# An S4 convolution and local attention kernel: its convolution kernel generated in quarters of the channels, from one written list of steps

## The chip, the core and the metric

The kernel runs on one core of a Trainium2 chip. The core has a matrix engine (PE, with a weight-load path shown as PEld), a vector engine (DVE), an activation engine (ACT), a general engine (POOL) and a sequencer that mostly issues DMAs (SP). Each engine works through its own queue in order; engines wait for each other through semaphores. On-chip memory is SBUF (128 partitions) and PSUM, where matmuls accumulate. The metric is device time in microseconds (us); smaller is better.

## The reference

Four layers on x of shape (1, 2048, 512), all bf16: S4 convolution, local attention, and both again with the same weights.

```python
def _A_ref(u, A_re, A_im, B_re, B_im, C_re, C_im, log_dt, Dskip):
    dt = jnp.exp(log_dt)[:, None]
    logdA = dt * (A_re + 1j * A_im)
    l = jnp.arange(L).astype(A_re.dtype)                      # bf16 positions
    P = jnp.exp(logdA[:, :, None] * l[None, None, :])
    K = jnp.einsum("dn,dnl,dn->dl", Cc, P, dt * Bc).real      # (512 channels, 2048 lags)
    y = irfft(rfft(pad(u)) * rfft(pad(K)))[:L]
    return y + u * Dskip

x = x + _A_ref(_layernorm(x), ...)
x = x + _B_ref(_layernorm(x), B_wqkv, B_wo)   # 32 heads, 8 keys at distance 0, 2, .., 14
x = x + _A_ref(_layernorm(x), ...)
x = x + _B_ref(_layernorm(x), B_wqkv, B_wo)
```

The positions are rounded to bf16, so that far lags fall together: the distinct ones are u + 8v with 21 values of u (`U_POS`) and 32 of v, and K at those is a product of two small tables of powers of lambda = exp(dt A).

## The kernel before, in words

The span has five parts: kernel generation (`kgen`), then for each of two layers the convolution (`a_layer`) and the attention (`b_layer`, whose order comes from a planner, `Plan`; it is not touched).

**Kernel generation.** `_kgen_ladder` (L564) makes lambda (`LAM`) and squares it eleven times: ACT squares (`sq`, L624), DVE makes the new imaginary (L632) and real part (L633, `lad`), ACT casts to bf16 (`L`, L626 to L629), with the eight instructions of C times B (`cb`) between. Each power is [128 modes, 2 parts, 512 channels].

Then two tables are built by doubling, for half of the channels at a time (256 channels, as 128 pairs): `Utab` (cb times lambda to the power u, steps 4, 2, 1, 256, 1024, 512, 2048) and `Vtab` (lambda to the power 8v, steps v2, v4, v8, v16, where step m makes entries m+1 to 2m-1 from 1 to m-1). `cmul` (L326) makes one step: four DVE products into `cp` (L336), then two sums. For half 0 most sums are made on PE (`add`, L487: identity matmuls into `psadd`, with a minus through `nident`) and evicted by ACT (L495); for half 1 the sums are DVE's (L345). The copies of powers into the tables (L417) and of cb (L383) are DVE's for half 0 and ACT's for half 1.

`products(c, U)` (L422) multiplies V by U for a quarter c of 128 channels: per pair of channels two matmuls of 64 weight columns by 42 (L432), real and imaginary part, and one per eight pairs that adds Dskip at lag 0 (L438). ACT casts the result to `KT` (L440); DMAs turn it to `rows` with lags on partitions (L446; eight per quarter, on SP for c of 0 and 1, half on POOL for 2 and 3).

`spectrum` (L452) multiplies rows by the constant `G`, in four blocks of 1024 frequencies and ten matmuls, for quarters 0 and 1; ACT casts to `ks` (L459), a DMA writes it to `kt_scratch` in DRAM. `spectrum_pairs` (L463), for quarters 2 and 3, uses that frequency f and its partner 1024 further differ in the sign of the odd lags alone: even lags (four matmuls) and odd lags (one) go to two banks, ACT copies the odd ones (L472), DVE writes sum and difference (L474).

The first layer norm's sums run on ACT, two passes of 16 rows (L175), spread through the steps; DVE applies it (L194).

**First stage and convolution, layer 0.** `first_stage` (L222) transforms the normed rows: two matmuls per row j against `F1` (L231), evicted to `Z` by ACT, for odd j half by DVE (L238 to L241). It takes turns with the last spectrum blocks on PE. `a_layer`'s loop then runs over 16 groups of 32 channels: transpose Z on PE (L202), evict `zt` on DVE (L207), second stage `xp` (L214), cast `xc` on ACT (L291), multiply by the spectrum `Kt` on DVE into `pab` (L298), inverse second stage `vp` on PE (L281), cast `VT` on ACT (L283). `load_k` (L260) loads Kt from `kt_scratch`, two DMAs of 256 KB per group on SP, into four buffers; group cg+4 is asked for after pab of cg. F1T (1 MB) is loaded on SP at the loop's start (L305). `y_rows` (L311) ends the convolution with `ps_y` matmuls (L317).

Order: outside the regions called `manual_schedule` a scheduler places the instructions; inside them, the order is that of the program text. Matmuls on the convolution's path wait for Z, Kt and PSUM buffers.

Of the kernel before, what the change touches and what calls it, by code (L numbers as in the profile page):

```python
# [12 lines left out]
ALU = mybir.AluOpType  # L13
# [54 lines left out]
P0 = U_POS.index(0)  # L68


def _kernel_dft():

    lag = np.arange(S)
    pos = lag.astype(np.float32).astype(NPBF).astype(np.int64)
    f = (np.arange(128)[None, :] * 2 + 1 + 512 * np.arange(16)[:, None]).reshape(-1)
    row = {}
    for s, u in enumerate(U_POS):  # L80
        for v in range(NV if s < NU - 1 else 1):
            row[u + 8 * v] = s * NV + v
    G = np.zeros((6 * 128, 2, S), dtype=np.float64)
    ang = -2 * np.pi * ((lag[:, None] * f[None, :]) % 8192) / 8192.0
    idx = np.array([row[p] for p in pos])
    np.add.at(G[:, 0, :], idx, np.cos(ang))
    np.add.at(G[:, 1, :], idx, np.sin(ang))
    G = G.reshape(6, 128, 4, 1024)
    return np.transpose(G[:5], (2, 1, 0, 3))
# [79 lines left out]
def first_norm_stats(nc, small, eps, Xg):  # L169

    st = {n: small.tile([128, NJ], F32, name="n1_" + n, bufs=1) for n in ("sum", "nmean", "m2", "den", "rstd", "nb")}
    junk = small.tile([128, D], BF, name="n1_junk", tag="junk", bufs=1)

    def row(j, func, out, **kw):
        nc.scalar.activation(junk[:], Xg[j // 4][:, j % 4, :], func, accum_out=st[out][:, j:j + 1], **kw)  # L175

    def ops():
        for j in range(NJ):
            yield row(j, ACT.Identity, "sum")
        nc.scalar.activation(st["nmean"][:], st["sum"][:], ACT.Copy, scale=-1.0 / D)  # L180
        for j in range(NJ):
            yield row(j, ACT.Square, "m2", bias=st["nmean"][:, j:j + 1])
        nc.scalar.activation(st["den"][:], st["m2"][:], ACT.Ln, bias=eps[:], scale=1.0 / D)
        nc.scalar.activation(st["rstd"][:], st["den"][:], ACT.Exp, scale=-0.5)
    return st, ops()


def first_norm_scale(nc, st):
    nc.vector.tensor_tensor(st["nb"][:], st["nmean"][:], st["rstd"][:], ALU.mult)


def first_norm_apply(nc, st, Xg, Ng):
    for j in range(NJ):
# [27 lines left out]

def first_stage(nc, tc, C, Ng, Z):  # L222

    turns = [C["psk_end"]] + [C["psg"][i][1] for i in range(8, 15)]
    nexts = {2 * i + 1: 8 + i for i in range(8)}
    with tc.tile_pool(name="a_ps1", bufs=2, space=PSUM, reuse_waits="tile") as ps1:
        for j in range(NJ):
            ps = ps1.tile([128, 2, D], F32, name="ps_s1", tag="ps1")
            with tc.issue_after(turns[j // 2].ins):
                for r in range(2):  # L230
                    mm = nc.tensor.matmul(ps[:, r, :], C["F1"][:, j, r, :], Ng[j // 4][:, j % 4, :], start=True, stop=True)  # L231
            if j in nexts:
                tc.add_manual_dep(C["psg"][nexts[j]][0].ins, mm.ins.name,
                                  mybir.DependencyInfo(mybir.DependencyClass.NoSync, mybir.DependencyReason.DATA),
                                  reason="spectrum and first stage by turns")
            src = ps[:].rearrange("k r (c e g) -> k r c g e", c=16, e=GE)
            if j % 2 == 1:
                nc.scalar.copy(z_view(Z)[:, 0, j], src[:, 0])  # L238
                nc.vector.tensor_copy(z_view(Z)[:, 1, j], src[:, 1])
            else:  # L240
                nc.scalar.copy(z_view(Z)[:, :, j], src)  # L241


def a_layer(nc, tc, C, Xg, Ng, kt_dram, load_w, Z, es_z):

    with ExitStack() as es:
        es.enter_context(es_z)
        layer = 0 if Z is None else 1
        def pool(name, bufs=1, es=es, **kw):
            return es.enter_context(tc.tile_pool(name=name, bufs=bufs, reuse_waits="tile", **kw))  # L250
        if layer == 0:
            Z = pool("a_z").tile([128, NGR, 128], BF, name="Z")
# [7 lines left out]
        def load_k(cg):  # L260
            Kt = fwork.tile([128, 8, 2, 128], BF, name="Kt", tag="Kt", bufs=4)
            rows = kt_dram.ap()[:, cg * 32:(cg + 1) * 32].rearrange("k (e g) a l -> k e (g a l)", e=GE)
            for h in range(2):
                nc.sync.dma_start(Kt[h::2].rearrange("q g a l -> q (g a l)"), rows)
            kts[cg] = Kt

        for cg in range(4):
            load_k(cg)
        if layer == 0:
            first_stage(nc, tc, C, Ng, Z)  # L270
# [15 lines left out]
        with tc.manual_schedule():  # L286
            for cg in range(-2, 18):
# [4 lines left out]
                if cg + 2 < 16:  # L292
                    zts[cg + 2] = z_transposed(nc, P, C, Z, (cg + 2) * 8)
# [32 lines left out]
def cmul(nc, tb, out, a, m, e, hn, add=None):  # L326

    cols = hn * e * 2  # L330
    prod = {}
    for i in range(2):
        for r in range(2):
            k = (i * 2 + r) * cols
            prod[i, r] = tb[:, k:k + cols]
            nc.vector.tensor_tensor(prod[i, r].rearrange("n (h e t) -> n h e t", h=hn, t=2), a(r),  # L336
                                    m[:, i].unsqueeze(2).to_broadcast([128, hn, e, 2]), ALU.mult)
    last = None
    for r, (x, y) in enumerate((((0, 0), (1, 1)), ((1, 0), (0, 1)))):
        o = out(r)  # L340
        if add is not None:
            add(r, prod[x], prod[y], o)
        else:
            x, y = (prod[k].rearrange("n (h f c) -> n h f c", h=hn, f=o.shape[2]) for k in (x, y))
            last = nc.vector.tensor_tensor(o, x, y, ALU.add if r else ALU.subtract)  # L345
    return last


def kgen(nc, tc, C, prm, kt_dram, load_rest, norm_stats, norm_apply):
    with ExitStack() as es:  # L350
        wk = es.enter_context(tc.tile_pool(name="k_work", bufs=1, reuse_waits="tile"))
        lp = es.enter_context(tc.tile_pool(name="k_powers", bufs=1, reuse_waits="tile"))
        vp = es.enter_context(tc.tile_pool(name="k_v", bufs=1, reuse_waits="tile"))
        gp = es.enter_context(tc.tile_pool(name="k_g", bufs=1, reuse_waits="tile"))
        Lb = {p: lp.tile([128, 2, D], BF, name=f"L{p}") for p in (1, 2, 4, 8, 16, 32, 64, 128, 256, 512, 1024, 2048)}
        cb = lp.tile([128, 2, D], BF, name="cb")
        V = vp.tile([128, DH2, 2, NV, 2], BF, name="Vtab")
        nc.gpsimd.memset(V[:, :, 0, 0, :], 1.0)
        nc.gpsimd.memset(V[:, :, 1, 0, :], 0.0)
        Gt = [gp.tile([128, 5, 1024], BF, name=f"G{b}") for b in range(3)]  # L360
        u0_es = ExitStack()
        up, late = [None, None], []

        def power(p, dsl):
            return Lb[p][:, :, dsl].rearrange("n r (h t) -> n r h t", t=2)

        with tc.tile_pool(name="k_prep", bufs=1) as pp:
            raw, load = load_raw(nc, pp, prm)
            _kgen_ladder(nc, tc, C, cb, Lb, pp, raw, load)
        g3 = es.enter_context(tc.tile_pool(name="k_g3", bufs=1, reuse_waits="tile"))  # L370
        Gt.append(g3.tile([128, 5, 1024], BF, name="G3"))
        load_rest()
        for b in range(4):
            nc.sync.dma_start(Gt[b][:], C["G_h"].ap()[b])
        kp = es.enter_context(tc.tile_pool(name="k_kp", bufs=2, reuse_waits="tile"))
        up[1] = es.enter_context(tc.tile_pool(name="k_u1", bufs=1, reuse_waits="tile"))
        up[0] = u0_es.enter_context(tc.tile_pool(name="k_u0", bufs=1, reuse_waits="tile"))
        cp = wk.tile([128, 8192], BF, name="cp")
        psk_pool = es.enter_context(tc.tile_pool(name="k_psk", bufs=2, space=PSUM, reuse_waits="tile"))

        def u_start(half):
            U = up[half].tile([128, DH2, 2, UW, 2], BF, name="Utab", tag="Utab")
            (nc.scalar.copy if half == 1 else nc.vector.tensor_copy)(U[:, :, :, P0, :].rearrange("n h r t -> n r h t"),  # L383
                                  cb[:, :, half * 2 * DCH:(half + 1) * 2 * DCH].rearrange("n r (h t) -> n r h t", t=2))
            return U

        def u_mul(half, U, p, src, dst, h0=0, h1=DH2, tb=cp, add=None):

            e = src[2]
            f = len(dst)  # L390
            step = dst[1] - dst[0] if f > 1 else e

            def a(r):
                return U[:, h0:h1, r, src[0]:src[0] + (e - 1) * src[1] + 1:src[1], :]

            def out(r):
                return U[:, h0:h1, r, dst[0]:dst[0] + f * step, :].rearrange(
                    "n h (f s) t -> n h f s t", s=step)[:, :, :, 0:e // f, :].rearrange("n h f s t -> n h f (s t)")
# [20 lines left out]

        quarters = ((0, DH2 // 2), (DH2 // 2, DH2))  # L420

        def products(c, U):  # L422

# [858 lines left out]
```

## Time and profile before

| what | us |
| --- | --- |
| median of 3 runs | 467.61 (467.24 to 468.58) |
| the profiled execution | 466.74 |
| its span, first to last instruction | 464.9 |
| busy in the span: PE, DVE, ACT | 386.4, 414.3, 335.2 |
| end of lambda (LAM) to the last spectrum output | 10.35 to 136.2 |
| first xc to first ps_y, layer 0 | 137.5 to 174.7 |
| the same in layer 1 | 307.58 to 341.11 |

The profile is one execution, recorded by hardware. Times of instructions are from the span's start. A group of instructions is told by its line, engine, operation and tiles with their busy time, count and mean duration, and then the idle time of the engine just before them with what ended it. A mean duration includes the last part in which the next instruction has begun already, so instructions that follow each other start at shorter distances than their durations. The granted clock of PE is a share of full speed.

### The profile page before, as it was taken

How to read it: one execution, taken by the hardware profiler on the slowest of the kernel's cores; microseconds unless marked ns; L12 is line 12 of the kernel's file. 1: busy time of each engine (PE TensorE's matmuls, PEld its weight loads, DVE VectorE, ACT ScalarE, POOL GpSimd, SP SyncE). 2: the span in 40 equal slices, each digit the busy share in tenths (PEclk: the TensorE clock that was granted, in tenths of full speed). 3: DMA queues.
4: the chain of work that ended last, by engine and by line, in shares of the span. 5: the costliest groups of instructions: out<-in, count | busy, mean ns of one | idle time of the engine just before them, and what ended most of it. 6: DMA issues, size and time to landing. Idle time of an engine off the chain costs nothing.

```text
span 464.9 us, 11615 instructions
## 1 busy us (share of the span) xinstructions
PE 386.4 (83%) x4692; PEld 259.1 (56%) x4731; DVE 414.3 (89%) x857; ACT 335.2 (72%) x579; POOL 19.4 (4%) x51
## 2 busy tenths in 40 slices
PE   2006789979977989999998899879988999988996
PEld 1002349466335864567776665347745567876662
DVE  4899999999786987879999999989879899999990
ACT  6987997984867898965665369969978656752354
POOL 3000000002300000001001000000000000110000
PEclk9999995878999899999999899999999999996899
DMA  8940001333579991002507007128700000456022
GB/s 237 420 159 0 1 1 17 83 69 83 137 170 276 274 287 36 3 3 59 102 1 161 2 1 221 54 52 273 222 0 5 1 1 3 99 103 118 1 92 92
DMA packets 36618, 45.56 MB, mean 98 GB/s; under 512 B 26660, under 2 KB 28068, under 8 KB 35668
## 3 DMA queue, kind: packets, MB, share of 16 engines
q1 hardware_dynamic: 34500, 41.00, 31.5%
q0 software_dynamic: 1248, 2.63, 2.6%
q10 hardware_dynamic: 816, 1.18, 0.7%
q8 instruction: 37, 0.61, 0.6%
q14 instruction: 17, 0.14, 0.1%
HBM read 30.55 MB, written 6.29 MB: 79 GB/s over the span
## 4 chain that ended last, share of the span: by engine, by line
PE 41%; DVE 31%; ACT 15%; issue 6%; DMA 5%; SPq 1%; DVEq 0%; ACTq 0%
PE ps_qk L900 10%; DVE prodpv L1054 9%; DVE cp L336 7%; DVE prodqk L929 4%; PE Lp L946 3%; ACT xc L291 3%; PE ps_v L961 3%; DMA Kt<-kt_scratch 3%; PE vp L281 3%; PE ps_o L1088 2%; PE pt L202 2%; PE xp L214 2%; ACT Z L1114 2%; PE po L1062 2%; DMA V<-V 2%
## 5 line engine op out<-in xcount | busy, mean ns | idle before, releaser
L929 DVE TENSOR_TENSOR prodqk<-qT,N 128x1024 bf16<-128x1024 bf16 (+3 forms) x176 | 83.8, 541 | 4.7 <-ACT qT L902 2.7
L1054 DVE TENSOR_TENSOR prodpv<-V,Lsb 128x1024 bf16<-128x1024 bf16 (+1 forms) x168 | 81.8, 558 | 0.2
L900 PE MATMUL ps_qk<-xnT,wqk 128*128 128x512 bf16 x256 | 61.4, 379 | 1.1 <-ACT xnT L886 1.1
L1062 PE MATMUL po<-halves,prodpv 128*128 128x64 bf16 x1024 | 48.4, 201 | 3.5 <-DVE prodpv L1054 2.0
L1062 PEld LDWEIGHTS <-prodpv 128*128 128x128 bf16 x1024 | 40.7, 103 | 17.3 <-DVE prodpv L1054 9.6
L298 DVE TENSOR_TENSOR pab<-xc,Kt 128x2048 bf16<-128x2048 bf16 x32 | 39.1, 1223 | 9.7 <-ACT xc L291 5.4
L493 PE MATMUL psadd<-cp,sb_ident 128*128 128x512 bf16 (+3 forms) x48 | 18.4, 383 | 33.2 <-DVE cp L336 30.2
L291 ACT CAST xc<-xp 128x1024 bf16<-128x1024 f32 x32 | 32.6, 1020 | 9.7 <-PE xp L214 6.8
L281 PE MATMUL vp<-sb_IC,pab 128*128 128x128 bf16 x512 | 34.4, 222 | 3.5 <-DVE pab L298 3.5
L900 PEld LDWEIGHTS <-wqk 128*128 128x128 bf16 x256 | 23.4, 97 | 23.3 <-DVE xnT L886 1.0
L283 ACT CAST VT<-vp 128x1024 bf16<-128x1024 f32 x32 | 32.4, 1021 | 4.9 <-PE vp L281 4.5
L1074 ACT CAST oT<-po 128x512 bf16<-128x512 f32 x32 | 17.6, 586 | 24.3 <-PE po L1062 24.3
L336 DVE TENSOR_TENSOR cp<-Vtab,L 128x896 bf16<-128x896 bf16 (+6 forms) x64 | 34.1, 597 | 0.7 <-PE psadd L494 0.4
L281 PEld LDWEIGHTS <-pab 128*128 128x128 bf16 x512 | 30.7, 99 | 5.0 <-DVE pab L298 4.0
L946 PEld LDWEIGHTS <-prodqk 128*128 128x128 bf16 x1024 | 30.9, 96 | 4.5
L961 PE MATMUL ps_v<-wv,xnT 128*128 128x256 bf16 x256 | 31.5, 272 | 0.0
L946 PE MATMUL Lp<-sb_bones,prodqk 128*128 128x8 bf16 x1024 | 31.0, 166 | 0.0
L336 DVE TENSOR_TENSOR cp<-Utab,L 128x256 bf16<-128x256 bf16 (+4 forms) x60 | 29.3, 546 | 1.0 <-PE psadd L494 0.8
L853 DVE BATCH_NORM_STATS2 ln_stats<-X 128x6 f32<-128x512 bf16 x37 | 23.7, 679 | 6.0 <-ACT X L1135 5.6
L432 PE MATMUL psk<-Utab,Vtab 128*64 128x42 bf16 x512 | 25.5, 208 | 4.1 <-DVE Vtab L345 2.5
L432 PEld LDWEIGHTS <-Vtab 128*64 128x64 bf16 x512 | 24.6, 138 | 6.8 <-issue 3.2
L968 ACT CAST V<-ps_v 128x512 bf16<-128x512 f32 x32 | 18.7, 587 | 12.1 <-PE ps_v L961 12.1
(174 smaller groups left out, 780.5 us busy)
## 6 DMA issues: line engine op xcount, KB each, us to landing
Kt<-kt_scratch SPq DMA_DIRECT2D x64, 256.0 KB, 4.5
G<-c_G SPq DMA_DIRECT2D x4, 1280.0 KB, 17.1
kt_scratch<-ks SPq DMA_DIRECT2D x12, 256.0 KB, 2.4
V<-V SPq DMA_DIRECT2D x8, 288.0 KB, 8.7
X<-in_A_u_dram SPq DMA_DIRECT2D x4, 512.0 KB
F1Tsb<-c_F1T SPq DMA_DIRECT2D x2, 1024.0 KB, 7.6
V<-V SPq DMA_DIRECT2D x4, 512.0 KB
V<-V POOLq DMA_DIRECT2D x4, 384.0 KB, 7.2
```

The costliest lines, as they stand in the source:

```text
L281: nc.tensor.matmul(vp[:, g, :], pab[:, g, ab, :], IC[:, ab, :], start=(ab == 0), stop=(ab == 1))
L283: nc.scalar.copy(dst.rearrange("k q (e g) -> k q e g", e=GE), vp[:].rearrange("k g (q e) -> k q e g", e=GE))
L291: nc.scalar.copy(xc[:].rearrange("q g o l -> q (g o l)"), xp)
L298: last = nc.vector.tensor_tensor(pab[:], xc[:].to_broadcast([128, 8, 2, 128]), kts[cg][:], ALU.mult)
L336: nc.vector.tensor_tensor(prod[i, r].rearrange("n (h e t) -> n h e t", h=hn, t=2), a(r), m[:, i].unsqueeze(2).to_broadcast([128, hn, e, 2] ...
L432: nc.tensor.matmul(ps[:, hl, 0:2 * NU], V[:, h, r, :, :].rearrange("n v t -> n (v t)"), U[:, h, r, 0:NU, :].rearrange("n u t -> n (u t)"), ...
L900: nc.tensor.matmul(t.ps[:], wqk[:, ct, f0:f0 + 128], x_group(g)[:, :, ct], start=(ct == 0), stop=(ct == 3))
L929: nc.vector.tensor_tensor(b.pr[:, u:u + 2 * n, 1 - a, :], cols(qT[i][:, ja * 128:(ja + n) * 128]), cols(kT[i][:, k0:k0 + n * 128]), ALU.mult)
L946: nc.tensor.matmul(t.Lp[:, w, u % 2, u // 2, :], b.pr[:, u].rearrange("f a q -> f (a q)"), bones[:], start=False, stop=(t.parts == W // 2 ...
L961: nc.tensor.matmul(t.ps[:, jj, :], tokens(ct, jp * 2 + jj, c), wv[:, ct, fp * 256:(fp + 1) * 256], start=(jj + ct == 0), stop=(jj == 1 and ...
L1054: nc.vector.tensor_tensor(t.p2[:, 0:nj, :].rearrange("p j (d h) -> p j d h", d=DH), m.V2[i // 2][:, c, r0:r0 + nj, f0:f0 + 128].rearrange( ...
L1062: nc.tensor.matmul(po[jj // k][:, jj % k, c, :], t.p2[:, jj, :], fold, start=(c == 0 and w == 0 and jj % k == 0), stop=(c == 1 and w == W ...
```

## The change

`KGEN` is a list of 327 names, and `kgen` now runs through it in one manual order, so that every engine's queue holds its instructions as the list has them. A name is a step: `m q l b` with a number are the ladder (imaginary part, square, real part, cast to bf16), `h x` the product C times B, `n` a row of the first norm (with `a`: on ACT), `r a` its rstd and its application, in halves; `u: A: B:` copies into the tables of a quarter (after the colon), `v8p:2` the DVE products of step v8 in quarter 2, `+v8p:2` their sum on PE, `=v8p:2` the eviction on ACT; without a `p` the sums stay on DVE. `p03` is the product V.U of quarter 0, fourth part, `k03` its cast to KT (and, after the last of four, the rows DMAs), `s e o` the spectrum's matmuls, ACT's and DVE's outputs (`o` is ACT, `e` is DVE), `f z` the first stage and its evictions to Z (`za` by ACT, `zv` by DVE, halves).

- Tables are built for quarters of 128 channels (64 pairs), in two buffers each of U and V; quarter c+2 waits for the products of quarter c. Where the access pattern allows, one DVE instruction multiplies both parts.
- Sums of all quarters go to PE and ACT, but for U512, one U4, v4 and U256. v16 (`n`) isn't summed at all: four DVE products go into `Vtab` and a second table (`Vsecond`), and the product V.U takes four matmuls per pair instead of two, two of them of 32 weight columns. Half a v16 in quarter 3 is summed on DVE.
- The spectrum keeps even and odd lags apart for all quarters, in blocks of 512 frequencies and their partners, and two of the four blocks of G go. For the first seven blocks (`PLUS`) PE adds the odd lags to the even ones, ACT writes this and twice the odd part, and DVE one difference. Dskip is added to the spectrum's real part there, on ACT or DVE.
- The first norm's row is done at once, on ACT (15 rows, with two small copies each) or DVE (one row).
- The first two zt evictions of layer 0 are ACT's. The first four Kt loads of layer 0 go to POOL's queue, after the last rows DMA. Half of all rows DMAs go to POOL.
- Z is reserved first, and its memory holds `cp` and low powers during the generation.

```diff
+KGEN = ("m0 q0 h0 l0 m1 q1 h1 l1 b0 x0 q2 x1 m2 b2 l2 b1 x2 x3 q3 m3 l3 b3 n4 q4 m4 l4 b4 x4 q5 x5 A:0 m5 A:1 t l5 u:0 b5 "
...
+        "v16yn:0 +0v8p:1 n12a =U2048p:0 +1v8p:1 U512:0 n3a =0v8p:1 =1v8p:1 p03 v16xn:0 +U2048p:1 n9a k03 p00 v16xn:1 U1p:1 "
+        "n10a k00 p02 =U2048p:1 +U1p:1 U512:1 =U1p:1 k02 p01 v16yn:1 n11a A:2 v2p:2 k01 p10 u:2 +v2p:2 B:2 k10 =v2p:2 U4:2 "
+        "U2p:2 p13 +U2p:2 n14a =U2p:2 v4:2 k13 p11 U256p:2 U2048p:2 n6a +U256p:2 =U256p:2 v8p:2 p12 U1p:2 u:3 +1v8p:2 n2a "
...
+        "U256:3 =0v8p:3 U1024p:3 =1v8p:3 p22 U1p:3 +U1024p:3 =U1024p:3 +U1p:3 k22 k23 s10 v16yn:3 =U1p:3 o10 p21 U512:3 s11 "
+        "e10 n0a k21 p32 n5a r0 s12 v16x:3 k32 o11 p33 o12 a0 k33 p30 e11 k30 e12 p31 f4 k31 s13 z4 f6 o13 f7 a1 z6 s20 e13 "
...
+        "e30 o31 f3 z11a z11v s32 z3 f13 e31 o32 f12 z13a z13v s33 z12 e32 o33 e33")
+PLUS = (0, 1, 2, 3, 4, 5, 6)
...
+            if name[-1] == "n":
+                W2 = W[c % 2]
+                for r, (dst, by) in enumerate(((T[:, :, 0], m[:, 0]), (W2[:, :, 0], Ln), (T[:, :, 1], m[:, 1]), (W2[:, :, 1], m[:, 0]))):
+                    nc.vector.tensor_tensor(dst[:, h0:h1, 0:e, :], T[:, h0:h1, r % 2, s0:s0 + e, :],
...
+        def sum_pe(name, c, rs):
+            prod, out, hn, f, size = sums[name, c]
+            ps = tiles["+", name, c, rs] = psum()[1].tile([128, 2, 512], F32, name="psadd", tag="psg")
...
+        def product(c, q):
+            ps = tiles["p", c, q] = psum()[0].tile([2 * NV, 16, 64], F32, name="psk", tag="psk")
+            parts = [(V[c % 2], r, slice(0, 2 * NV)) for r in range(2)]
+            if "v16" + "xxyy"[q] + f"n:{c}" in everything:
+                parts[1:1] = [(W[c % 2], r, slice(0, NV)) for r in range(2)]
...
+        def spectrum(c, i):
+
+            ps = tiles["s", c, i] = psum()[1].tile([128, 2, 512], F32, name="psg", tag="psg")
+            g = Gt[i // 2][:, :, (i % 2) * 512:(i % 2 + 1) * 512]
+            even = range(5) if 4 * c + i in PLUS else range(4)
+            for bank, lags in enumerate((even, range(4, 5))):
+                for t in lags:
+                    nc.tensor.matmul(ps[:, bank, :], tiles["rows", c][:, t, :], g[:, t, :], start=(t == lags[0]), stop=(t == lags[-1]))
...
+            free = [f"p{c - 2}{q}" for q in range(4)] if c >= 2 else []
...
+                    word("+" + tag + full, lambda name=name, c=c, rs=rs: sum_pe(name, c, rs), full, "x5")
+                    word("=" + tag + full, lambda name=name, c=c, rs=rs: sum_out(name, c, rs), "+" + tag + full)
...
-        for cg in range(4):
-            load_k(cg)
-        if layer == 0:
-            first_stage(nc, tc, C, Ng, Z)
+        with tc.issue_after(C["rows_end"].ins) if layer == 0 else nullcontext():
+            for cg in range(4):
+                load_k(cg, nc.gpsimd if layer == 0 else nc.sync)
...
-                    zts[cg + 2] = z_transposed(nc, P, C, Z, (cg + 2) * 8)
+                    zts[cg + 2] = z_transposed(nc, P, C, Z, (cg + 2) * 8, layer == 0 and cg < 0)
```

## The prediction

> **What bounds the kernel now.** The change rewrites the kernel generation and the first layer's stage after it, so I first ask which stretch of the span those are, and which engine has no slack in them. The busy times by stretch (length; then PE, weight loads, DVE, ACT and POOL, each busy us with a count; granted PE clock; DMA share; GB/s):
>
> ```profile
> 10.35:36.30 25.95, 0.00 (x0) 0.00 (x0) 23.99 (x53) 23.81 (x31) 0.00 (x0) 1.00 0.69 277
> 36.30:65.50 29.20, 22.86 (x122) 10.12 (x125) 27.84 (x56) 25.44 (x47) 0.00 (x0) 1.00 0.00 1
> 65.50:111.00 45.50, 39.97 (x456) 27.94 (x461) 45.22 (x92) 35.88 (x78) 2.33 (x4) 0.74 0.23 47
> 111.00:136.20 25.20, 22.76 (x225) 12.22 (x226) 21.18 (x42) 19.77 (x29) 3.55 (x12) 1.00 0.61 143
> 10.35:136.20 125.85, 85.59 (x800) 50.28 (x809) 118.23 (x239) 104.90 (x183) 5.88 (x16) 0.91 0.35 103
> 137.50:174.70 37.20, 30.09 (x390) 25.09 (x395) 30.00 (x34) 30.46 (x32) 0.00 (x0) 0.95 0.95 277
> 307.58:341.11 33.53, 28.59 (x393) 23.83 (x396) 29.95 (x34) 30.27 (x32) 0.00 (x0) 1.00 0.62 189
> ```
>
> From the end of the first power of lambda (10.35) to the last spectrum output (136.2) DVE works 118.2 of 125.85 us: it is the bound, with 7.6 us idle, of which 4.0 lie after 111. The last two rows are the spectral products of layer 0 and layer 1, the same code from the first xc to the first ps_y matmul: 37.2 us against 33.5. The waits say why (waiter, releaser, total, times, longest; the second line is the only long wait that layer 1 has not):
>
> ```profile
> DVE lad L633 <- ACT sq L624: 1.9, 1, 1.9
> ...
> DVE pab L298 <- DMA Kt<-kt_scratch: 3.9, 1, 3.9
> ```
>
> The groups give the prices (busy, mean ns of one):
>
> ```profile
> L336 DVE TENSOR_TENSOR cp<-Utab,L 128x1024 bf16<-128x1024 bf16 x16 | 10.1, 686 | 0.8 <-PE psadd L494 0.8
> ...
> L336 DVE TENSOR_TENSOR cp<-Vtab,L 128x1920 bf16<-128x1920 bf16 x8 | 8.7, 1152 | 0.0
> ...
> L474 DVE TENSOR_TENSOR ks<-psg,odd 128x512 bf16<-128x512 f32 x8 | 5.5, 692 | 1.3 <-ACT odd L472 1.3
> ```
>
> A mean holds some 0.08 us in which the next instruction has begun: four of 1024 start within 2.48 us (0.61 each), four of 1920 within 4.36 (1.08). I use start to start: 0.07 us + 0.52 ns per element for bf16 tables (512: 0.335, 768: 0.47, 960: 0.57, 1536: 0.87, 1792: 1.0), 0.27 for 256 in runs of two, 0.60 for 512 of f32 or from PSUM.
>
> Last, PE's clock (same columns as above):
>
> ```profile
> 68.00:70.00 2.00, 0.51 (x17) 0.44 (x14) 2.00 (x6) 2.00 (x6) 0.00 (x0) 1.00 0.00 0
> 70.00:72.00 2.00, 1.87 (x45) 1.87 (x45) 2.00 (x4) 1.67 (x5) 0.00 (x0) 0.71 0.04 8
> 72.00:74.00 2.00, 2.00 (x42) 2.00 (x40) 2.00 (x4) 1.52 (x4) 0.00 (x0) 0.50 0.00 0
> ...
> 112.00:114.00 2.00, 2.00 (x69) 2.00 (x67) 2.00 (x7) 1.47 (x3) 0.00 (x0) 1.00 0.78 178
> ```
>
> The products V.U (42 columns each) run 69 in 2 us at full clock and 42 at half, and fall to half although PE is never idle: 33 ns each against 53 ns. It costs nothing now, because DVE is behind.
>
> **The change, part by part.** DVE first.
> Products of the tables: the work per element is the same, but with four quarters and both parts of a complex number in one instruction there are fewer and longer ones. Per quarter: v2 and U4 and U2048 2x0.27 each, v4 2x0.47, v8 2x1.0, v16 8x0.57, U2 2x0.335, U1 and U256 2x0.60 each, U1024 4x0.27, U512 2x0.87; four quarters give 59.7 us (before, by the same prices, 60.2). No gain.
> Sums: before, half 0 had three steps and half 1 all its steps summed on DVE, 16.6 us. After, only U512 (8x0.47), U4, v4 in quarter 2, U256 and a half of v16 in quarter 3: 6.5 us. -10.1.
> Table copies: half 1's ran on ACT; now all are on DVE, 12 of them, 3.8 instead of 1.75. +2.1.
> Spectrum outputs: even and odd lags are now apart for all 16 blocks, not 8 of them. Seven blocks have PE add the odd lags once too much (ACT writes the sum, DVE one instruction), nine take two: 25x0.605 = 15.1 instead of 16x0.605 = 9.7. +5.4.
> Z evictions 6 instead of 8 (-1.2), one row of the first norm on DVE (+0.7), the ladder's 30 instructions of 0.6 unchanged.
> Sum 113.0 instead of 116.5 by the same prices; the measured 118.2 is 1.5% over 116.5, so 114.7 after: -3.5.
>
> DVE's idle time is the unknown. At the start the table load and two copies that ACT did ahead of the first square go elsewhere, and with them the 1.9 us wait. From there the work looks like 36.3 to 65.5, DVE product, PE sum, ACT eviction, next step: 4.7% idle. After the first norm's rstd (the step r0) it looks like 111 to 136, three engines in turn: 16% idle. Of the 113.0 us, 88.5 stand before r0 in the list: 88.5x1.015/0.953 = 94.2; the other 24.5x1.015/0.84 = 29.6. End of the stage: 10.35+94.2+29.6 = 134.2 instead of 136.2. -2.0. The ends: if all went like 65.5 to 111 (0.6% idle), 10.35+115.4 = 125.8, -10.4; if all went like the last stretch, 10.35+136.5 = 146.9, +10.7.
>
> ACT, by start-to-start prices: squares and casts of the ladder 21.4, evictions of sums 25.2 (37 evictions at 0.1 us + 0.79 ns per element of each half), 16 KT casts 9.9, odd lags 11.5, Z 12.2, 15 norm rows of 0.62+0.72 and two small copies of 0.2 each (bounds 0.12, an n_nmean to its successor, and 0.34, an n_den to its dependent successor) 26.1, rest 2.8: 109.1, ending no earlier than 119.5. It is hidden by DVE's 134.2; each 0.1 on the small copies is 3.0 us of its slack of 14.7.
>
> PE: the last V products now go unsummed, so a product has 64 matmuls and not 34. By 33 ns that is 2.1 us instead of 1.1, 31 us in all instead of 17; the table sums 19.6 (47 thousand columns at 0.215 us per 512), spectrum 18.6 instead of 25.8, first stage 7. In sum 76 of 124 us, hidden while the clock is full; what if it is not is the first rival. The second table's matmuls have 32-column weights, which no row shows: the ends are 24.5 ns (the 128x8 Lp matmuls) and 53 ns, I take the 33 of their neighbours.
>
> Queues: G's loads halve (2.6 MB, nobody waits for them). The rows DMAs of quarters 0 and 1 move four each from SP to POOL, 0.6 us per issue; SP gets 32 writes of kt_scratch for 16, at 0.36 to 0.53 us some 7 us more over 60, still a fifth of its time. The first four Kt loads (8 DMAs, 0.57 us issue each on POOL's own rows) go to POOL, behind the last rows DMA, some 17 us before the stage ends; on SP, four of the eight came after 132 and F1T behind them. The four buffers lie over tables that are done by then. So the 3.9 us wait goes: layer 0 takes what layer 1 takes, 33.5 instead of 37.2: -3.65. Ends: nothing (F1T is still issued at the loop's start and 4 MB must move in the last 17 us) and -3.65. I take the whole, since layer 1 with early loads is the nearest row. The first two zt evictions go to ACT, and the list ends with z12 e32 o33 e33, so Z is complete while DVE still has two spectrum outputs to write: I leave the distance from the stage's end to the first xc as it is, 1.3 us.
>
> Sum: the profiled execution took 466.74 us (span 464.9 and 1.84 around it), 0.87 under the median 467.61. 466.74-2.0-3.65 = 461.1; with the 0.87, 461.9.
>
> A rule is set against a row here. Row: before the fall at 70.7 the longest PE gap was 1.62 us, and PE was then busy 2.00 of 2 us at clock 0.50 until 84. The Trainium skill, "TensorE: Matmul & The Clock Gate", section "Why this matters for your kernels", asks only for no idle gaps over about 3 us to keep the clock. By that rule the products here would stay at full clock and 461.9 would need no rival on PE; by the row sparse products lose it, and the trace doesn't agree with the rule. So:
>
> **Rival 1: PE becomes the bound, slower.** Place: the eight products of quarters 0 and 1, from p03 until quarter 3's tables may be written (u:3). The two table buffers mean that quarter 2 waits for all products of quarter 0, quarter 3 for those of quarter 1. DVE has 20.1x1.015/0.953 = 21.4 us there. PE has 8x64 matmuls and 2.6 us of sums: 19.5 us at 33 ns, but 8x3.4+5.1 = 32.4 at half clock. Price 11 us: 472.9. It decides from 27.1 us on (the whole gain of 5.7), about six tenths of that stretch at half clock. For it: the fall at 70.7, and that at 98 again; sums are dense but short there. Against: 60.8 to 68 and 111.6 to 116, products among sums or behind a dense spectrum, stayed at 1.00.
>
> **Rival 2: the Kt wait stays**, moved to F1T or to the kt_scratch writes that share the DMA engines (1.05 busy at 132 to 135): 461.9+3.65 = 465.5.
>
> **Rival 3: the list packs as tightly as half 1's tables did.** The stage ends at up to 125.8, 8.4 us earlier: 453.5; halfway 457.7. For it: norm rows are spread as filler for ACT. Against: ACT at 109 and DVE at 115 us leave little to fill with.
>
> **How the numbers follow.** Forecast 461.9 (own range 458.5 to 466): 0.36. Rival 1 in full 0.22, in part (some 4 us, 466) 0.12. Rival 2: 0.10. Rival 3: 0.20. Three tenths of a per cent is about what a measurement can tell. Faster: 0.36+0.10+0.20 and a third of 0.12, less a little for the forecast's upper end: 0.68. Same 0.07, slower 0.25. The range leaves out the last tenth of rivals 3 and 1: 454.5 to 472.
>
> **What would show it.** Right: the last e step's DVE output near 134, DVE busy near 115 from 10.4 on, no DMA line among pab's waits in layer 0 and 33 to 34 us from the first xc to the first ps_y. Wrong: PE at 0.50 and busy 2 of 2 us between the first product and quarter 3's tables, with DVE's table products released by PE or ACT there; or pab waiting for Kt; or DVE idle over 15 us with ACT over 95% busy, which would mean that ACT is the bound.

## The result: 14% slower, and the profile after

The changed kernel takes 533.29 us (median, 531.25 to 534.55) where the kernel before took 467.43 beside it: a ratio of 1.141, 95% interval 1.135 to 1.147. The forecast was 461.9 with a range up to 472. The profiled execution has a span of 529.5 us instead of 464.9. Three executions that stood far above the rest of their kernel (1870.92 us with the Kt loads on SP, 471.74 in passes, and 472.23 of the kernel before) are left out of the ratios here and below, but not out of the medians.

The stage that was forecast to end at 134.2 ends at 203.9. These are the busy times by stretch of the changed kernel (columns as for the kernel before: length; PE, weight loads, DVE, ACT, POOL; granted PE clock; DMA share; GB/s):

```profile
10.35:203.90 193.55, 162.07 (x1234) 100.28 (x1246) 119.54 (x228) 113.85 (x246) 13.69 (x26) 0.73 0.21 61
60.00:80.00 20.00, 19.78 (x179) 14.09 (x179) 5.13 (x8) 7.13 (x19) 0.00 (x0) 0.50 0.01 2
80.00:110.00 30.00, 29.78 (x270) 21.38 (x270) 10.68 (x23) 9.61 (x27) 2.33 (x4) 0.50 0.04 7
```

DVE's work in the stage is what it was (119.5 us against 118.2), but between 60 and 110 DVE works 15.8 of 50 us, ACT 16.7, and PE 49.6. The bound has moved to PE. The chain of the work that ended last names what PE does there (start, length, what):

```profile
60.93 13.25 PE psk L481 x128
76.00 13.25 PE psk L481 x128
89.80 6.68 PE psk L481 x64
...
125.37 5.30 PE psk L481 x64
```

These are V.U products with the second table, 64 matmuls each: 6.68 us at clock 0.50, 5.30 at clock 1.00 (but for the end of the latter: from 130.0 to 130.7 the clock was 0.57). That is 104 and 83 ns per matmul, where the forecast had 53 and 33. The waits show what stood behind them (waiter, releaser, total, times, longest):

```profile
ACT KT L489 <- PE psk L481: 31.7, 9, 6.1
ACT Utab L472 <- PE psadd L463: 23.7, 6, 7.3
...
DVE Vtab L582 <- PE psk L481: 16.6, 1, 16.6
...
DVE Utab L579 <- PE psk L481: 9.3, 1, 9.3
DVE ks L532 <- ACT odd L522: 8.3, 1, 8.3
```

The two long DVE waits are the table copies of quarters 2 and 3 (A:2 and u:3), which may be written only when the products of quarters 0 and 1 are done: the place that rival 1 named. The prediction's sign of being wrong, PE at 0.50 and busy nearly all the time until quarter 3's tables, is there.

Why a matmul takes that long can be seen when the start times within a product are listed (start, length of the row, what, count; the clock is 1.00 here):

```profile
125.30 0.21 PE L481 MATMUL psk<-Utab,Vtab 128*64 128x42 bf16 x1
125.44 0.22 PE L481 MATMUL psk<-Utab,Vsecond 128*32 128x42 bf16 x2
125.59 0.24 PE L481 MATMUL psk<-Utab,Vtab 128*64 128x42 bf16 x2
125.76 0.22 PE L481 MATMUL psk<-Utab,Vsecond 128*32 128x42 bf16 x2
125.91 0.24 PE L481 MATMUL psk<-Utab,Vtab 128*64 128x42 bf16 x2
126.08 0.22 PE L481 MATMUL psk<-Utab,Vsecond 128*32 128x42 bf16 x2
```

The matmuls come in twos of one width: by the length of the rows, the second starts some 0.03 us behind the first. Whenever the stationary tile (the operand that PE holds, here the part of the V table) goes from 64 columns (`Vtab`) to 32 (`Vsecond`) or back, the next two start 0.15 to 0.17 us behind the two before. The order that the code writes (V, W, W, V for each channel pair) changes the width twice per pair, 32 times per product, and 14 of the 16 products have a second table.

So there are three theories. **Theory 1**: each change of width costs PE about 0.1 us. **Rival A**: tiles of 32 columns are slow in themselves. **Rival B**: it is the lost clock alone (at 53 ns, rival 1 came to 472.9).

### The profile page after: what moved, and what is told of

Its sections match the earlier page's. It is cut to its first block, busy times and chain, and to the rows that moved or that the text cites. A ratio compares the mean times of both kernels' runs of the same rounds, so it can differ in the third digit from the quotient of the medians.

```text
span 529.5 us, 12564 instructions
## 1 busy us (share of the span) xinstructions
PE 463.1 (87%) x5124; PEld 308.6 (58%) x5166; DVE 414.7 (78%) x845; ACT 343.9 (65%) x642; POOL 28.3 (5%) x69
## 4 chain that ended last, share of the span: by engine, by line
PE 58%; DVE 17%; ACT 14%; issue 5%; DMA 4%; SPq 1%; DVEq 0%; ACTq 0%
PE psk L481 17%; PE ps_qk L953 8%; DVE prodpv L1107 8%; ACT xc L272 4%; PE psg L508 3%; PE pt L209 3%; PE ps_v L1014 3%; PE ps_o L1141 3%; PE Lp L999 3%; DVE prodqk L982 3%; PE po L1115 2%; PE vp L262 2%; PE xp L221 2%; DMA V<-V 2%; DMA kt_scratch<-ks 2%
## 5 line engine op out<-in xcount | busy, mean ns | idle before, releaser
L481 PE MATMUL psk<-Utab,Vtab 128*64 128x42 bf16 x512 | 68.8, 224 | 0.6 <-DVE Utab L448 0.6
L481 PE MATMUL psk<-Utab,Vsecond 128*32 128x42 bf16 x448 | 54.8, 204 | 0.2 <-DVE Utab L448 0.2
L481 PEld LDWEIGHTS <-Vtab 128*64 128x64 bf16 x512 | 42.5, 135 | 18.0 <-issue 6.8
L462 PE MATMUL psadd<-Z,sb_ident 128*128 128x128 bf16 (+3 forms) x70 | 26.5, 392 | 28.2 <-DVE Z L441 19.7
L1115 PE MATMUL po<-halves,prodpv 128*128 128x64 bf16 x1024 | 47.3, 202 | 3.8 <-DVE prodpv L1107 2.3
L262 PE MATMUL vp<-sb_IC,pab 128*128 128x128 bf16 x512 | 33.5, 219 | 1.5 <-DVE pab L279 1.4
L264 ACT CAST VT<-vp 128x1024 bf16<-128x1024 f32 x32 | 32.4, 1021 | 3.7 <-PE vp L262 3.7
L481 PEld LDWEIGHTS <-Vsecond 128*32 128x32 bf16 x448 | 27.7, 104 | 9.9 <-issue 0.6
L489 ACT CAST KT<-psk 64x672 bf16<-64x672 f32 x16 | 11.4, 718 | 31.7 <-PE psk L481 31.7
L472 ACT CAST Utab<-psadd 128x256 bf16<-128x256 f32 (+2 forms) x44 | 15.8, 420 | 23.9 <-PE psadd L463 23.7
```

What stands on the lines that cost most here:

```text
L262: nc.tensor.matmul(vp[:, g, :], pab[:, g, ab, :], IC[:, ab, :], start=(ab == 0), stop=(ab == 1))
L264: nc.scalar.copy(dst.rearrange("k q (e g) -> k q e g", e=GE), vp[:].rearrange("k g (q e) -> k q e g", e=GE))
L462: nc.tensor.matmul(ps[:, b, 0:s.stop - c0], C["ident"][:], prod[0][:, r, s], start=True, stop=False)
L481: nc.tensor.matmul(ps[lanes, hl, 0:2 * NU], T[:, q * 16 + hl, r].rearrange("n v t -> n (v t)"), U[c % 2][:, q * 16 + hl, r, 0:NU].rearrang ...
L1115: nc.tensor.matmul(po[jj // k][:, jj % k, c, :], t.p2[:, jj, :], fold, start=(c == 0 and w == 0 and jj % k == 0), stop=(c == 1 and w == W ...
```

## Experiments on the products

**The same matmuls in passes.**

```diff
+ passes = [parts[0:1], parts[1:3], parts[3:4]] if len(parts) == 4 else [parts]
- for hl in range(16):
-     for i, (T, r, lanes) in enumerate(parts):
+ for h0 in range(0, 16, 16):
+     for some in passes:
+         for hl in range(h0, h0 + 16):
+             for T, r, lanes in some:
...
```

> The matmuls of a product with the second table are the same, in another order: the first V row of all 16 pairs, both second-table rows of all 16 pairs, the second V row of all 16 pairs; PE goes 2 times instead of 32 between stationary tiles of 64 and of 32 columns. Theory 1 (going from one width to the other costs PE about 0.1 us each time): a product takes 64 x 33 ns + 2 x 0.1 = 2.3 us at full clock instead of 5.3 (at half clock 64 x 53 ns + 0.2 = 3.6 instead of 6.7), and the kernel falls to the forecast's region, 462 to 473 us. Rival A (stationary tiles of 32 columns are slow in themselves, some 127 ns each): order is no matter, 533 us. Rival B (the lost PE clock alone): order is no matter, 533 us.

465.01 us, ratio to the kernel before 0.993 (0.991 to 0.996). The order alone takes 68 us off. Rivals A and B, for which order was no matter, fall. The chain of this kernel shows products of 3.12 us at half clock (two of them in the first line) and 2.13 at full:

```profile
57.53 6.24 PE psk L485 x128
...
69.68 2.13 PE psk L485 x64
```

**Half the changes of width.**

```diff
+ for h0 in range(0, 16, 2):
+     for some in passes:
+         for hl in range(h0, h0 + 2):
...
```

> As the run before, but in groups of two pairs: 16 goings between widths per product, half of the changed kernel's 32. Theory 1: 1.6 us less per product (3.7 instead of 5.3 us at full clock, 5.0 instead of 6.7 at half), 14 products, so some 22 us less: 505 to 515 us, about halfway to the run before. Rivals A and B: 533 us.

496.73 us, ratio 1.064 (1.061 to 1.068): between the two, though lower than I expected. The products:

```profile
59.27 9.51 PE psk L485 x128
...
110.89 3.56 PE psk L485 x64
```

With 32, 16 and 2 changes of width the same 64 matmuls take 5.30, 3.56 and 2.13 us at full clock: 1.74/16 = 0.109 and 1.43/14 = 0.102 us per change. At half clock 6.68, 4.76 (9.51/2) and 3.12: 0.120 and 0.117. The price is linear in the number of changes, and nearly the same at both clocks. 14 products x 30 changes make 43 to 50 us. The two profiled executions are 64.4 us apart (529.5 and 465.1), and PE's busy time in the stage differs by as much (162.1 and 97.4). The clock stays at 0.50 from 56 to 116 in the changed kernel and is back at 64 in the kernel with passes, and that goes with the other 14 to 22 us: the table sums are 6.1 us longer (31.3 against 25.2, group means of 402 to 415 ns instead of 329 to 336) and the spectrum's matmuls 3.7 (26.7 against 23.0). Some seven more products at half clock, 1.0 us longer each (3.12 against 2.13), would add 7; this last part is an estimate.

**Tiles of 32 columns only.** Each V row becomes two matmuls, for lanes 0 to 31 and 32 to 63 (lanes are the partitions of the product in PSUM). A product has 96 matmuls, none of 64 columns.

```diff
- parts = [(V[c % 2], r, slice(0, 2 * NV)) for r in range(2)]
+ low, high = slice(0, NV), slice(NV, 2 * NV)
+ parts = [(V[c % 2], r, low, 0) for r in range(2)]
...
- parts[1:1] = [(W[c % 2], r, slice(0, NV)) for r in range(2)]
+ parts[1:1] = [(W[c % 2], r, low, 0) for r in range(2)]
+ parts += [(V[c % 2], r, high, NV // 2) for r in range(2)]
```

> Every stationary tile of a product has 32 columns: each V row is two matmuls, for lanes 0 to 31 and 32 to 63, so a product with the second table has 96 matmuls and PE never goes from one width to another, but 32 times from one lane half to the other. Theory 1 (width): 96 x 25 to 33 ns = 2.4 to 3.2 us a product at full clock, 462 to 480 us. Theory 1b (any change of the tile's place or width costs 0.1 us): 96 x 25 ns + 32 x 0.1 = 5.6 us, 533 to 545 us. Rival A (127 ns per 32-column tile): 12 us a product, over 600 us.

463.40 us, ratio 0.992 (0.988 to 0.995). Half as many matmuls again, and the products are shorter still. The chain and the starts within one product:

```profile
67.59 1.51 PE psk L484 x82
```

```profile
69.72 0.18 PE L484 MATMUL psk<-Utab,Vsecond 128*32 128x42 bf16 x1
69.74 0.18 PE L484 MATMUL psk<-Utab,Vtab 128*32 128x42 bf16 x1
69.74 0.18 PE L484 MATMUL psk<-Utab,Vsecond 128*32 128x42 bf16 x1
69.77 0.22 PE L484 MATMUL psk<-Utab,Vtab 128*32 128x42 bf16 x3
69.82 0.18 PE L484 MATMUL psk<-Utab,Vsecond 128*32 128x42 bf16 x1
```

Six matmuls (a channel pair) start every 0.10 us, 17 ns each, and going from one lane half to the other costs nothing that can be seen. It is the width that costs, not the place (theory 1b falls). Nor is it that four matmuls in a row add to the same place in PSUM, which the order in passes had largely undone: in the narrow kernel's program four in a row still add to lanes 0 to 31. The Trainium skill, "TensorEngine Tiling (Array Packing)", section "Key Properties", says that changing the tiling mode, not just the tile, drains TensorE. The runs agree in that only the change of width costs time, and give the price that the page doesn't: 0.10 to 0.12 us. I had not weighed that page in the forecast.

**No second table.** The last V steps are summed on DVE, so a product has 32 matmuls of 64 columns. (Two of those steps, for quarter 0, take scratch space over products of quarter 1's v8 and U2048 that PE has yet to sum, so some table entries are other numbers; instructions and sizes are those of the full work.)

```diff
- "v16yn:0 +0v8p:1 n12a =U2048p:0 +1v8p:1 U512:0 n3a =0v8p:1 =1v8p:1 p03 v16xn:0 +U2048p:1 n9a k03 p00 v16xn:1 U1p:1 "
+ "v16y:0 +0v8p:1 n12a =U2048p:0 +1v8p:1 U512:0 n3a =0v8p:1 =1v8p:1 p03 v16x:0 +U2048p:1 n9a k03 p00 v16x:1 U1p:1 "
...
```

> The last V steps sum on DVE everywhere, so no product has second-table matmuls (32 matmuls of 64 columns each). DVE has 7 halves x 2 sums x 0.57 us = 8 us more, less 7 x 2 x 0 (the four products stay). Theory 1 and rival A both: PE's products fall to 32 x 33 ns = 1.1 us, DVE is the bound again: 461.9 + 8 = 470, give or take 5. Rival B (clock alone): products at 32 x 53 ns = 1.7 us, also near 470. What this run tells is what the other 46 us are: if it stays above 500, the second table isn't the cause.

472.87 us, ratio 1.013 (1.008 to 1.017). DVE is busy 125.8 us in the stage, 7.6 above the kernel with narrow tiles, as counted (8). So the second table is worth 8 to 9 us (472.9 against 465.0 in passes, where the tiles of `Vtab` have 64 columns too, and 463.4 in the narrow kernel), once its matmuls are cheap. PE's clock is at 0.50 from 54 to 76 here too, without a change of width in the products, and DVE's idle time in the stage is 9.5 us against the narrow kernel's 7.9: the lost clock by itself costs little here, not 60 us.

## Experiments on the Kt loads

With cheap products the stage can be held against the forecast. In the narrow kernel layer 0's loop takes 33.5 us from the first xc (136.7) to the first ps_y (170.2), as forecast, but the stage ends at 136.4, not 134.2. DVE's waits there and the last stretch:

```profile
DVE ks L535 <- DMA kt_scratch<-ks: 3.1, 1, 3.1
DVE Z L549 <- ACT Z L551: 2.7, 3, 1.2
```

```profile
10.35:136.40 126.05, 86.66 (x1747) 52.37 (x1759) 118.17 (x228) 112.58 (x246) 14.29 (x26) 0.97 0.32 94
...
115.00:135.00 20.00, 16.38 (x75) 7.00 (x75) 13.10 (x21) 14.80 (x23) 4.18 (x9) 0.91 0.77 202
```

DVE is idle for 6.9 of the last 20 us, and the chain has one link of 8.40 us in which a `ks` buffer waits to be written out. The early Kt loads were issued from 115 to 119, and move 2 MB in the same stretch. The edits of this section are made to the narrow kernel.

**The Kt loads back on SP.**

```diff
- with tc.issue_after(C["rows_end"].ins) if layer == 0 else nullcontext():
-     for cg in range(4):
-         load_k(cg, nc.gpsimd if layer == 0 else nc.sync)
+ for cg in range(4):
+     load_k(cg)
```

> The kernel with 32-column tiles only (463.4 us; layer 0's loop 33.5 us from the first xc to the first ps_y matmul, stage end 136.4), with the first four Kt loads put back on SP, where the kernel before has them. Forecast's term: the 3.65 us wait for Kt comes back, loop 37.2 us, time 467. Rival (the early loads cost what they give, since they hold up the kt_scratch writes that the last spectrum outputs wait for, 3.1 us of DVE and 8.4 us of the chain): loop 37 but the stage ends 3 us earlier, time 463 to 464. A third case: no Kt wait in spite of SP, 460.

464.33 us, ratio 0.994 (0.990 to 0.997), not to be told from the narrow kernel's 0.992. Its waits and the first rows of its loop:

```profile
DVE pab L278 <- DMA Kt<-kt_scratch: 5.4, 5, 3.0
DVE Z L548 <- ACT Z L550: 1.5, 3, 0.5
```

```profile
L271 ACT CAST xc<-xp x32: 1012/1018/1045, 131.9 to 333.0; 128x1024 bf16<-128x1024 f32 x32
L297 PE MATMUL ps_y<-VT,F1Tsb x32: 376/379/379, 170.0 to 347.8; 128*128 128x512 bf16 x32
```

The loop begins 4.8 us earlier and lasts 4.6 us longer (38.1), so the first ps_y comes at 170.0 instead of 170.2. The rival holds: what the early loads give the loop they take from the stage.

**A fifth ks buffer.**

```diff
- ks = late["kp"].tile([128, 2, 512], BF, name="ks", tag="ks", bufs=4)
+ ks = late["kp"].tile([128, 2, 512], BF, name="ks", tag="ks", bufs=5)
```

> The kernel with 32-column tiles only, with five buffers for ks instead of four: DVE writes one block of the spectrum more ahead of the kt_scratch writes that leave it. Theory (the 3.1 us DVE wait for kt_scratch<-ks sets the stage's end, for want of a buffer): wait down to 0 to 2, the stage ends 1 to 3 us earlier, 460.5 to 462.5. Rival (the DMA engines are full there, busy share 1.05 at 120 to 125, and the same bytes must move before the loop): the wait is found again at pab's Kt or in the loop, 463.4.

459.80 us, ratio 0.985 (0.981 to 0.988). The stage ends at 134.0, the loop takes 33.6 us, and the wait is down to this:

```profile
DVE ks L533 <- DMA kt_scratch<-ks: 0.4, 1, 0.4
```

**Two of the four loads early.**

```diff
  with tc.issue_after(C["rows_end"].ins) if layer == 0 else nullcontext():
-     for cg in range(4):
+     for cg in range(2):
          load_k(cg, nc.gpsimd if layer == 0 else nc.sync)
+ for cg in range(2, 4):
+     load_k(cg)
```

> The kernel with 32-column tiles only, with two of the four early Kt loads left on POOL and the other two on SP behind the kt_scratch writes: 1 MB less moves while the last blocks are written. Theory (the early loads hold up the writes): DVE's 3.1 us wait falls to 1 or less, the stage ends 2 to 3 us earlier, and the loop takes 33.5 to 35.5, since pab wants the third Kt 4 us after its start: 460.5 to 465. Rival (the writes are slow by themselves): wait stays 3, loop gets longer by up to 2: 463.4 to 465.5.

460.14 us, ratio 0.984 (0.980 to 0.988): the same wait goes (0.4 us left), by the other way. pab waits 1.3 us for Kt, and the loop stays at 33.6. Both ways together:

> The kernel with 32-column tiles only, with five ks buffers and with two early Kt loads: the two edits that gave 459.8 and 460.1 alone, without the change to quarter 3's V table. If they take away the same wait for kt_scratch (3.1 us of DVE), they do not add up: 459 to 461 us, last spectrum output near 133. If each takes away its own: 457 to 458.

459.68 us, ratio 0.984 (0.981 to 0.988). They take away the same wait and do not add up. And with the last half of quarter 3's V table unsummed as well (`v16x:3` becomes `v16xn:3`):

> The kernel with 32-column tiles only, with five ks buffers, two early Kt loads, and the last half of quarter 3's V table unsummed as well (2 DVE sums of 0.57 us less, two products of 96 instead of 64 matmuls). If the parts add up: stage end 3 to 4 us earlier than 136.4, loop 33.5 to 35.5, 459 to 462 us. If DVE's idle time at the end is set by PE and ACT instead: 463.

463.27 us, ratio 0.991 (0.987 to 0.994). Against the run above it differs only in that half. DVE has two sums less, but the last KT cast comes at 115.3 instead of 112.4, and DVE then waits in one piece for ACT's `odd`:

```profile
DVE ks L537 <- ACT odd L527: 3.0, 1, 3.0
```

An edit that relieves the busiest engine made the kernel slower, by 3.0 us by the ratios and 3.6 by the medians; the two intervals just touch. Why the cast comes later isn't shown.

## An experiment on the clock

In all kernels above with 64-column tiles a part of the products ran at half clock; in the first narrow kernel they ran at 1.00. So I cut the tiles of the kernel before in two:

```diff
- for r in range(2):
-     nc.tensor.matmul(ps[:, hl, 0:2 * NU], V[:, h, r, :, :].rearrange("n v t -> n (v t)"),
+ for v0 in (0, NV // 2):
+     for r in range(2):
+         nc.tensor.matmul(ps[2 * v0:2 * v0 + NV, hl, 0:2 * NU], V[:, h, r, v0:v0 + NV // 2, :].rearrange("n v t -> n (v t)"),
...
```

> The kernel before, with the stationary tile of each V.U product cut into two of 32 columns (64 matmuls of 32 columns and 2 of 64 for the skip per product, where it has 32 of 64 and 2). DVE is its bound, so the time should stay at 467 either way. Told apart by PE's clock: if it is the width of the tile that lets the clock fall, the stretches 70 to 84 and 98 to 110 stay at 1.00 and a product takes 64 x 18 ns + 0.2 = 1.4 us; if it is that products stand between stretches of idle or half-empty PE, the clock falls to 0.50 there as before.

468.43 us, ratio 1.005 (1.002 to 1.008): as expected no gain, since DVE is the bound. First the stretch of the kernel before in which the clock falls, then the kernel with cut tiles (its profiled execution is the longest of its ten, 472.50 us):

```profile
70.00:84.00 14.00, 12.92 (x210) 11.49 (x211) 14.00 (x23) 10.52 (x26) 0.00 (x0) 0.53 0.11 17
```

```profile
68.00:80.00 12.00, 9.37 (x454) 8.26 (x446) 12.00 (x25) 11.94 (x30) 0.00 (x0) 1.00 0.09 16
80.00:86.00 6.00, 3.16 (x8) 1.19 (x9) 5.96 (x11) 2.59 (x7) 0.00 (x0) 0.51 0.12 17
```

The products run at 1.00 now, but the clock falls right behind them, where PE is half idle, and is at 0.57 between 104 and 108. Nor do narrow tiles always keep the clock: of the six narrow kernels above, two ran all products of quarters 0 and 1 at 1.00 (the first one, and the one with the loads on SP), and in the other four most of the first two products ran at half clock. With five `ks` buffers and two early loads the clock fell at 54.2, just as the products began (0.56 from 54.3 to 58.0, 1.00 from 58.0 on), and six matmuls then started every 0.14 us instead of 0.10. So the width of the tile alone doesn't decide it. What it is that the clock follows, these runs don't tell.

## Why the prediction was wrong, step by step

**The step that failed: PE's cost.** "The second table's matmuls have 32-column weights, which no row shows", with ends of 24.5 and 53 ns, and "I take the 33 of their neighbours". They measured 83 ns at full and 104 ns at half clock as a mean over the product, outside both ends. The ends came from rows in which all matmuls of a run have one width; the change interleaves two. I had bounded the price of the new instruction and not that of its place between instructions of another width. 14 products x 32 changes x 0.1 us = 45 us were left out, and with them and the lost clock "76 of 124 us, hidden" became 162 us of PE in a stage of 193.5. In the narrow kernel, with neither, PE is busy 86.7 us.

**Rival 1 had the bound and the place, but not the cause.** It named PE as the bound of the eight products of quarters 0 and 1, from p03 until u:3, by the lost clock alone. It gave 32.4 us for them; they ran from 54.1 to 112.6, 58.5 us, at clock 0.50. Without the changes of width its 472.9 didn't come about either: in passes (465.0) three products ran at half clock, at 3.1 us where the rival had 3.4, and then the clock came back. What the rival says against a fall of the clock (two stretches of products in the kernel before that stayed at 1.00) was a weak argument: 56 to 116 ran at 0.50.

**The clock rule.** The prediction set a row against what the Trainium skill, "TensorE: Matmul & The Clock Gate", section "Why this matters for your kernels", asks for: no idle gaps over about 3 us. This trace doesn't agree with that rule either: the longest gap of PE between 42 and the fall at 55 was 1.81 us, and the clock then stayed at 0.50 while PE was busy 49.6 of 50 us. The busy share doesn't tell the clock: in the narrow kernel PE was busy 8.4 of 10 us between 54 and 64 at 1.00, against 10.0 of 10 at 0.50 in passes, where the half clock itself makes the same work longer.

**DVE's work, -3.5: wrong, it was -0.1** (118.17 in the narrow kernel's stage, 118.23 before). By the sums of the groups, the table products cost 3.8 us more (67.2 for 63.4; I had -0.5) and the table copies 4.0 more (6.0 for 2.0; I had +2.1); the table sums -11.1 (-10.1), the spectrum outputs +6.1 (+5.4), Z -1.4 (-1.2) and the norm row +0.9 (+0.7) were near. The misses are in the forms with short runs: products of 256 elements that start 0.35 us apart (431 to 438 ns as group means, 380 to 386 in the kernel before), for which I took 0.27, and copies of 768 at 810 ns. (Group sums count the overlap of neighbours, 9.6 us in all before and 11.3 in the narrow kernel, so the rises are somewhat smaller than they look. The prediction's list of product prices adds up to 60.0, not 59.7.)

**DVE's idle time, stage end 134.2: the number met by luck.** With cheap products the stage ends at 136.4. With a fifth buffer, which the forecast didn't have, it ends at 134.0, but of 118.4 us of work and 5.2 idle, not 114.7 and 9.1: two errors that nearly cancel.

**The Kt wait, -3.65: right for the loop, wrong for the sum.** The loop takes 33.6 us in the changed kernel and 33.5 in the narrow one. But I took the stage before it as untouched by the loads, and the same loads hold up the kt_scratch writes by as much. I had named those writes among the Kt wait's rivals only as a delay to the loop, not to DVE's last outputs.

**ACT hidden at 109: right** (112.6 us in a stage of 126). With the order of the matmuls put right the change gives 463.4 to 465.0 where 461.9 was forecast, or 459.7 with the writes out of the way: 1.6% under the kernel before. That the sum of the rest came so near is in part luck, since DVE's work was set 3.4 us too low and its idle time too high.

## What to carry to other kernels

Order small matmuls so that those with stationary tiles of one width stand together, or cut them all to one width: here a change between 64 and 32 columns cost as much as three to six matmuls of 42 columns. When a change mixes instructions that the old trace shows only apart, the price of the mixture has to be bounded by itself; the old rows bound it from below only. And when transfers are moved earlier, look up what else waits on the DMA engines at that time: the next buffer to come free may be the path that sets the end.

## What I had not expected of the hardware

A change of the stationary tile's width on PE, between 64 and 32 columns, costs 0.10 to 0.12 us at either clock; going from one lane half to the other at the same width costs nothing that can be seen. At full clock, matmuls of 42 columns start every 17 ns with 32-column tiles in two lane halves, and every 33 ns with 64-column tiles: 96 of the first are done sooner (82 in 1.51 us) than 64 of the second (2.13 us).
